# Layer 1 of a two-layer kernel in 13 chunks of 488 and 416 tokens instead of 14 chunks of 448

## The chip, the cores and the metric

The kernel runs on one core of one Trainium2 chip. The metric is the device time of one execution in microseconds (us); the number compared is the median of several runs. Beside the runs there is one execution with the hardware profiler on.

## The reference, cut to what matters

Two samples of 3136 tokens with 256 features go through three stages, one after the other:

```
scores = z @ z.T / 3136;  x = u * (max(scores, 0)**2 @ v)        # attention, no softmax
u = x + (x.T @ U @ V).T;  x = u + max(u @ w1a, 0) @ w2a          # layer 1, U and V of rank 32
u = x + real(fft2(x));    n = (u - mean) / sqrt(var + 1e-6)      # layer 2
out = u + max(n @ w1b, 0) @ w2b
```

The hidden width is 1024. All is float32. U, V and the four weight matrices come as 64-bit floats and are turned into 32-bit ones on the chip.

## The kernel before

Tokens and features stand in an order made on the host, so that the Fourier transform over 3136 = 64 x 49 tokens splits into small matmuls. Features lie on partitions (two halves of 128, called a), tokens along the free dimension. To keep float32 accuracy, every operand is split into a high part h and a remainder l (types that one pass of TensorE takes), and a product is three matmuls: high x high, high x low, low x high.

**Attention** (function `attention`, lines 423 to 826) walks over 14 query chunks of 448 tokens and 13 key blocks each. Its PSUM pools are given back at its end. The jobs that turn 64-bit numbers into 32-bit ones (`words`, line 158) run beside it. The first chunk of layer 1 is prepared in its last steps (`first_chunk`, line 706; lines 808 to 814).

**Layers 1 and 2** (lines 832 to 1187) are one loop over 28 chunks of 448 tokens: layer 1, sample 0, chunks 0 to 6; sample 1, chunks 0 to 6; then the same for layer 2. Each chunk has 8 steps, one for each 128 hidden units, and the loop variable i counts the 224 steps (line 1148). In step i `hidden` (line 363) does six matmuls for the chunk's hidden block (lines 368 to 370), ScalarE takes the ReLU (373) and VectorE the remainder (374). `project` (line 378) does the six matmuls back to 256 features (393 to 395) for the step two before, so that two steps lie between. Nothing is scheduled by the compiler here: the order of the program is the order on each engine's queue (`manual_schedule`).

What has to be done beside this is written as generators that advance once in every step, or as single calls at listed steps:

- `prep1` (line 260) and `prep2` (line 299) get the next chunk ready; they are put in at step 2 of a chunk's 8 for layer 1 and step 0 for layer 2 (line 1163). `prep1` does two matmuls of the low-rank term (269), adds the tokens (270) and splits the sum. `load` (252) brings the V columns of a chunk by two DMAs on the POOL queue.
- `mixer` (866) forms the rank-32 sums of sample 1, with the sample's own tile as a staging buffer.
- `halves49` (895) has four parts for each eighth of a sample: `fold`, `fetch`, `tokens` and `axis49`, at the steps of lines 1138 to 1143. `fold` reads tokens that layer 1 has finished.
- `fourier` (960) does the rest of the transform of one sample and adds it to the tokens. It starts at step 65 for sample 0 and 121 for sample 1 (line 1131), and rests in step 0 of each chunk. Line 1164 asserts that it is over when the first layer-2 chunk of its sample is prepared.
- `convert` (1092) turns the second layer's weights; `weights2` (1117) brings the second half of them in, from step 107.

DMAs go out on three queues: SP (`load`), POOL (`late_dma`) and, at few places, ACT. Attention writes its output to DRAM, and `load_x` (863) brings it back into the tiles `xT` (one for each sample, line 840) at the steps of lines 1146 and 1147.

## Time and profile before

| | |
|---|---|
| median of 3 runs | 1132.9 us (1132.52 to 1133.41) |
| the profiled execution | 1132.07 us |
| its span, first to last instruction | 1130.3 us |
| TensorE (PE) busy | 1125.1 us |
| VectorE (DVE) busy | 847.0 us |
| ScalarE (ACT) busy | 633.7 us |
| GpSimd (POOL) busy | 181.5 us |
| attention, to the first matmul of layer 1 | 536.7 us |
| layer 1, to the first matmul of layer 2 | 298.3 us |

All times inside the span count from its start. PE is the matmul itself, PEld the load of its weights, which runs beside other matmuls. A matmul's printed duration is modelled and overlaps the next one. A row of the timeline gives start, length, engine, line, operation, tiles (written <- read) and shape; "x6" at its end says that six like instructions were merged.

### The profile page before, as it was taken

What the parts mean: (1) busy time and instruction counts of PE and PEld (TensorE: products, weight loads), DVE (VectorE), ACT (ScalarE), POOL (GpSimd) and SP (SyncE); (2) the same over time, 40 slices, a digit from 0 to 9 for tenths busy, and PEclk for the clock granted to TensorE, in tenths of its full rate; (3) what the DMA queues carried; (4) which work ended last, traced back from release to release, by engine and by line L of the source; (5) the groups of instructions that cost most, each with busy time, mean ns of one, the idle gap of its engine ahead of it and who ended that gap; (6) DMA issues with size and microseconds to landing.
All of it is one profiled execution on the core that took longest, in us unless ns stands there. A gap on an engine that the chain in (4) does not pass through costs nothing.

```text
span 1130.3 us, 21424 instructions
## 1 busy us (share of the span) xinstructions
PE 1125.1 (100%) x8310; PEld 1061.7 (94%) x8310; DVE 847.0 (75%) x1571; ACT 633.7 (56%) x1032; POOL 181.5 (16%) x299
## 2 busy tenths in 40 slices
PE   9999999999999999999999999999999999999998
PEld 8999999999999999999989999999999999999997
DVE  8877888888887667676667777577588888777863
ACT  8777777878786666675334444343345444444431
POOL 2202310221022102202221112111131100000010
PEclk9999999999999999999999999999999999999999
DMA  5212322324123302111823455231143321111111
GB/s 168 75 46 61 104 80 69 119 71 127 47 72 118 121 18 59 50 36 32 265 62 95 128 159 130 74 75 45 47 107 100 76 48 42 33 42 33 42 33 42
DMA packets 86758, 88.96 MB, mean 79 GB/s; under 512 B 27398, under 2 KB 76034, under 8 KB 86656
## 3 DMA queue, kind: packets, MB, share of 16 engines
q1 hardware_dynamic: 70272, 58.44, 17.2%
q0 software_dynamic: 16032, 28.93, 10.2%
q8 instruction: 65, 1.06, 0.4%
q14 instruction: 37, 0.30, 0.1%
q10 hardware_dynamic: 352, 0.21, 0.1%
HBM read 57.67 MB, written 29.82 MB: 77 GB/s over the span
## 4 chain that ended last, share of the span: by engine, by line
PE 99%; ACT 0%; DVE 0%; issue 0%; DVEq 0%; POOL 0%; POOLq 0%
PE psO L616 37%; PE psS L574 9%; PE psH L368 8%; PE psH L369 8%; PE psC L394 8%; PE psC L395 8%; PE psH L370 8%; PE psC L393 8%; PE psS L743 0%; PE ps_m L995 0%; PE ps_g L995 0%; PE ps_x L995 0%; PE psS L234 0%; PE ps_g L234 0%; PE ps_m L958 0%; PE ps_m L957 0%
## 5 line engine op out<-in xcount | busy, mean ns | idle before, releaser
L616 PE MATMUL psO<-h,Vt 64*128 64x448 f32 x2744 | 345.1, 363 | 0.2 <-DVE h L585 0.2
L616 PEld LDWEIGHTS psO<-h,Vt 64*128 64x128 f32 x2744 | 294.4, 185 | 9.1 <-DVE h L585 0.7
L93 DVE TENSOR_TENSOR l<-P,h 128x896 fp32r<-128x896 f32 (+2 forms) x237 | 224.8, 954 | 33.3 <-ACT h L90 16.4
L373 ACT ACTIVATE Hh<-psH 128x448 fp32r<-128x448 f32 x224 | 121.0, 541 | 201.5 <-PE psH L370 198.3
L374 DVE SCALAR_TENSOR_TENSOR Hl<-psH,Hh 128x448 fp32r<-128x448 f32 x224 | 138.3, 620 | 117.9 <-ACT Hh L373 115.7
L590 ACT ACTIVATE P<-psS 128x896 f32<-128x896 f32 (+1 forms) x181 | 160.2, 885 | 85.4 <-PE psS L574 84.6
L616 PE MATMUL psO<-l,Vt 64*128 64x448 f32 x1372 | 206.4, 363 | 0.0
L592 DVE CAST h<-P 128x896 fp32r<-128x896 f32 (+1 forms) x181 | 110.9, 613 | 85.0 <-ACT P L591 83.8
L591 ACT ACTIVATE P<-P 128x896 f32<-128x896 f32 (+1 forms) x181 | 167.4, 925 | 5.7
L368 PE MATMUL psH<-h,w 128*128 128x448 f32 x448 | 166.5, 372 | 0.0
L616 PEld LDWEIGHTS psO<-l,Vt 64*128 64x128 f32 x1372 | 159.9, 185 | 4.4 <-DVE l L93 0.3
L369 PE MATMUL psH<-l,w 128*128 128x448 f32 x448 | 163.4, 365 | 0.0
L394 PE MATMUL psC<-Hl,w 128*128 128x448 f32 x448 | 163.4, 365 | 0.0
L370 PE MATMUL psH<-h,w 128*128 128x448 f32 x448 | 162.9, 364 | 0.0
L393 PE MATMUL psC<-Hh,w 128*128 128x448 f32 x448 | 162.9, 364 | 0.0
L395 PE MATMUL psC<-Hh,w 128*128 128x448 f32 x448 | 162.7, 363 | 0.0
L574 PE MATMUL psS<-Q,KT 64*128 64x448 f32 x1002 | 147.6, 364 | 0.0
L574 PEld LDWEIGHTS psS<-Q,KT 64*128 64x128 f32 x1002 | 115.2, 185 | 3.7 <-issue 0.4
L368 PEld LDWEIGHTS psH<-h,w 128*128 128x128 f32 x448 | 84.3, 188 | 7.9 <-issue 0.3
L393 PEld LDWEIGHTS psC<-Hh,w 128*128 128x128 f32 x448 | 84.2, 188 | 6.8 <-issue 0.2
L370 PEld LDWEIGHTS psH<-h,w 128*128 128x128 f32 x448 | 84.2, 188 | 6.5
L394 PEld LDWEIGHTS psC<-Hl,w 128*128 128x128 f32 x448 | 84.2, 188 | 6.3 <-DVE Hl L374 0.5
(313 smaller groups left out, 1157.1 us busy)
## 6 DMA issues: line engine op xcount, KB each, us to landing
out<-P SPq DMA_DIRECT2D x27, 224.0 KB, 1.9
uT<-in_uT SPq DMA_DIRECT2D x13, 448.0 KB, 4.0
aTd<-aT POOLq DMA_DIRECT2D x13, 448.0 KB, 3.1
aNd<-aT POOLq DMA_DIRECT2D x104, 56.0 KB, 2.4
vraw<-in_v SPq DMA_DIRECT2D x18, 256.0 KB, 2.7
scr<-wst SPq DMA_DIRECT2D x16, 256.0 KB, 2.0
Vs<-Vd POOLq DMA_DIRECT2D x28, 112.0 KB, 2.6
xT<-aTd SPq DMA_DIRECT2D x7, 448.0 KB, 4.6
```

The source lines that it names most:

```text
L93: tt(out=o, in0=a, in1=b, op=ALU.subtract)
L368: mm(ps[:, 0:CH], wh, self.h[:, a], start=a == 0, stop=False)
L369: mm(ps[:, 0:CH], wh, self.l[:, a], start=False, stop=False)
L370: mm(ps[:, 0:CH], wl, self.h[:, a], start=False, stop=a == 1)
L374: stt(out=l, in0=ps[:, 0:CH], scalar=0.0, in1=f(h), op0=ALU.max, op1=ALU.subtract)
L393: mm(dst, wh, h, start=k == 0, stop=False)
L394: mm(dst, wh, l, start=False, stop=False)
L395: mm(dst, wl, h, start=False, stop=k == 7)
L574: mm(dst[:, 0:w], k, q[r, kq, o : o + w], start=(kk, kq) == (0, 0), stop=kk == 1)
L590: act(out=A[:, x].rearrange("p (a n) -> p a n", a=2), in_=ps[:, :, 0:w], func=AF.Relu, scale=1.0 / S)
L591: act(out=A[:, x], in_=A[:, x], func=AF.Square)
L616: mm(o[fa][i][:, 0:CH], vt[r, j, k, fa * 128 : fa * 128 + 128], x[r, j * CH : j * CH + CH], start=p == 0 and fa not in [t[1][0] for t in t ...
```

## The change

Layer 1 takes both samples as one row of 6272 tokens and cuts it into 13 chunks, twelve of 488 and the last of 416. Chunk 6 holds the last 208 tokens of sample 0 and the first 280 of sample 1; its low-rank term is two matmuls for each half of the features, and its V columns come by four DMAs. Layer 2 keeps its 14 chunks of 448.

Both samples lie in one tile X, of which `xT` are views. Tiles that hold a chunk grow from 448 to 488 columns a half. For that, room is made elsewhere: the exponent of `words` is written into the lowest 16 bits of each 64-bit word instead of a separate stretch, the staging tiles shrink from 1152 to 1024 words, and the tiles `top`, `alt` and one of the two `wst` buffers move into the tile of U, which is free by then.

Layer 1 has 104 steps instead of 112. `fourier(0)` stays at step 65, `fourier(1)` moves from 121 to 113 and `weights2` from 107 to 99. The steps of the folds are listed one by one: for sample 0 they were 14, 22, 30, 38, 46, 54, 57, 58 and for sample 1 70, 78, 86, 94, 102, 110, 113, 114.

```diff
@@ -21,6 +21,8 @@
 N1, N2 = 64, 49
 CH = 448
 NC = S // CH
+CW = 488
+L1 = -(-NB * S // CW)
 NP = 13
 KPOS = 25
 
...
@@ -98,13 +100,13 @@
     dram = ctx.enter_context(tc.tile_pool(name="dram", bufs=1, space=DRAM))
 
     def ctile(tag, dt=F32, **k):
-        return com.tile([128, 2 * CH], dt, tag=tag, name=tag, **k)
+        return com.tile([128, 2 * CW], dt, tag=tag, name=tag, **k)
 
     def ptile():
         return ctile("P", bufs=4)
 
-    def c2(t):
-        return t.rearrange("p (a n) -> p a n", a=2)
+    def c2(t, n=CH):
+        return t.rearrange("p (a n) -> p a n", a=2)[:, :, 0:n]
 
     def run(gen):
         for _ in gen:
...
@@ -161,7 +163,7 @@
         hi = w.rearrange("p (n w) -> p n w", w=2)[:, :, 1]
         r16 = w.bitcast(U16).rearrange("p (n w) -> p n w", w=4)
         s, m = (raw[0:np_, k * n : k * n + n] for k in (2, 3))
-        e = raw[0:np_, 4 * n : 4 * n + n // 2].bitcast(U16)
+        e = r16[:, :, 0]
         nc.vector.tensor_scalar(out=e, in0=r16[:, :, 3], scalar1=0x7FF0, scalar2=None, op0=ALU.bitwise_and)
         nc.vector.tensor_scalar(out=m, in0=hi, scalar1=0xFFFFF, scalar2=None, op0=ALU.bitwise_and)
         yield
...
@@ -247,27 +249,36 @@
     class Chunk:
         def __init__(self, layer, b, c):
             self.layer, self.b, self.c = layer, b, c
-            self.sl = slice(c * CH, c * CH + CH)
+            t0 = b * S + c * CH if layer == 2 else c * CW
+            self.n = CH if layer == 2 else min(CW, NB * S - t0)
+            self.sl = slice(t0, t0 + self.n)
+            self.parts = []
+            for q in range(NB):
+                s, t = max(t0, q * S), min(t0 + self.n, q * S + S)
+                if s < t:
+                    self.parts.append((q, slice(s - t0, t - t0), slice(s - q * S, t - q * S)))
 
         def load(self):
-            self.vs = com.tile([128, CH], F32R, tag="Vs", name="Vs", bufs=1)
+            self.vs = com.tile([128, CW + 8], F32R, tag="Vs", name="Vs", bufs=1)
             for k in (0, 64):
-                late_dma(out=self.vs[k : k + 64, :], in_=V_d[:, self.sl])
+                for _, here, there in self.parts:
+                    late_dma(out=self.vs[k : k + 64, here], in_=V_d[:, there])
 
         def prep(self):
             return self.prep1() if self.layer == 1 else self.prep2()
 
         def prep1(self):
-            b, vs = self.b, self.vs
-            a = late["xT"][b][:, :, self.sl]
-            yield
-            if self.c or self.b:
+            n, vs = self.n, self.vs
+            a = late["X"][:, :, self.sl]
+            yield
+            if self.c:
                 yield
-            x, h, l = c2(ptile()), c2(ctile("h", F32R)), c2(ctile("l", F32R))
+            x, h, l = c2(ptile(), n), c2(ctile("h", F32R), n), c2(ctile("l", F32R), n)
             for k in range(2):
                 ps = misc()
-                mm(ps[:, 0:CH], Gs[b][:, k * 128 : k * 128 + 128], vs, start=True, stop=True)
-                tt(out=x[:, k], in0=ps[:, 0:CH], in1=a[:, k], op=ALU.add)
+                for b, here, _ in self.parts:
+                    mm(ps[:, here], Gs[b][:, k * 128 : k * 128 + 128], vs[:, here], start=True, stop=True)
+                tt(out=x[:, k], in0=ps[:, 0:n], in1=a[:, k], op=ALU.add)
                 hcopy(h[:, k], x[:, k])
                 sub(l[:, k], x[:, k], f(h[:, k]))
                 yield
...
@@ -362,16 +373,17 @@
 
         def hidden(self, k):
             w, mp = late["w"][self.layer][0], late["mp"]
-            ps = late["psH"].tile([128, 512], F32, tag="H", name="psH")
+            n = self.n
+            ps = late["psH"].tile([128, 512], F32, tag="H", name="psH")[:, 0:n]
             for a in range(2):
                 wh, wl = w.first(k, 0, a), w.first(k, 1, a)
-                mm(ps[:, 0:CH], wh, self.h[:, a], start=a == 0, stop=False)
-                mm(ps[:, 0:CH], wh, self.l[:, a], start=False, stop=False)
-                mm(ps[:, 0:CH], wl, self.h[:, a], start=False, stop=a == 1)
-            h = mp.tile([128, CH], F32R, tag="Hh", name="Hh", bufs=3)
-            l = mp.tile([128, CH], F32R, tag="Hl", name="Hl", bufs=3)
-            act(out=h, in_=ps[:, 0:CH], func=AF.Relu)
-            stt(out=l, in0=ps[:, 0:CH], scalar=0.0, in1=f(h), op0=ALU.max, op1=ALU.subtract)
+                mm(ps, wh, self.h[:, a], start=a == 0, stop=False)
+                mm(ps, wh, self.l[:, a], start=False, stop=False)
+                mm(ps, wl, self.h[:, a], start=False, stop=a == 1)
+            h = mp.tile([128, CW], F32R, tag="Hh", name="Hh", bufs=3)[:, 0:n]
+            l = mp.tile([128, CW], F32R, tag="Hl", name="Hl", bufs=3)[:, 0:n]
+            act(out=h, in_=ps, func=AF.Relu)
+            stt(out=l, in0=ps, scalar=0.0, in1=f(h), op0=ALU.max, op1=ALU.subtract)
             self.hid = getattr(self, "hid", {})
             self.hid[k] = (h, l)
 
...
@@ -389,7 +401,7 @@
                     parts.insert(1, self.held)
             for a, k, h, l in parts:
                 wh, wl = w.last(k, 0, a), w.last(k, 1, a)
-                dst = self.acc[a][:, 0:CH]
+                dst = self.acc[a][:, 0 : self.n]
                 mm(dst, wh, h, start=k == 0, stop=False)
                 mm(dst, wh, l, start=False, stop=False)
                 mm(dst, wl, h, start=False, stop=k == 7)
...
@@ -400,7 +412,12 @@
             b = self.b
             if self.layer == 1:
                 for a in range(2):
-                    tt(out=late["xT"][b][:, a, self.sl], in0=self.acc[a][:, 0:CH], in1=self.x[:, a], op=ALU.add)
+                    tt(
+                        out=late["X"][:, a, self.sl],
+                        in0=self.acc[a][:, 0 : self.n],
+                        in1=self.x[:, a],
+                        op=ALU.add,
+                    )
             else:
                 o = c2(ptile())
                 if self is chunks[-1]:
...
@@ -415,9 +432,9 @@
                     tt(out=o[:, a], in0=self.acc[a][:, 0:CH], in1=self.rs, op=ALU.mult)
                 for a in range(2):
                     tt(out=o[:, a], in0=o[:, a], in1=self.x[:, a], op=ALU.add)
-                    load(out=out[b, a * 128 : a * 128 + 128, self.sl], in_=o[:, a])
-
-    chunks = [Chunk(y, b, c) for y in (1, 2) for b in range(NB) for c in range(NC)]
+                    load(out=out[b, a * 128 : a * 128 + 128, self.c * CH : self.c * CH + CH], in_=o[:, a])
+
+    chunks = [Chunk(1, 0, c) for c in range(L1)] + [Chunk(2, b, c) for b in range(NB) for c in range(NC)]
 
 
     def attention(stack):
...
@@ -706,15 +725,16 @@
         def first_chunk(a):
 
             ch = chunks[0]
-            x = c2(ptile())
+            n = ch.n
+            x = c2(ptile(), n)
             for k in range(2):
                 ps = psS.tile([128, 2, 512], F32, tag="S", name="psS")
                 for i, r in enumerate(halves):
-                    mm(ps[:, i, 0:CH], Gs[0][r, k * 128 : k * 128 + 128], ch.vs[r], start=True, stop=True)
+                    mm(ps[:, i, 0:n], Gs[0][r, k * 128 : k * 128 + 128], ch.vs[r, 0:n], start=True, stop=True)
                 for i, y in enumerate((a, x)):
-                    tt(out=x[:, k], in0=ps[:, i, 0:CH], in1=y[:, k], op=ALU.add)
-            yield
-            h, l = c2(ctile("h", F32R)), c2(ctile("l", F32R))
+                    tt(out=x[:, k], in0=ps[:, i, 0:n], in1=y[:, k], op=ALU.add)
+            yield
+            h, l = c2(ctile("h", F32R), n), c2(ctile("l", F32R), n)
             for k in range(2):
                 hcopy(h[:, k], x[:, k])
                 sub(l[:, k], x[:, k], f(h[:, k]))
...
@@ -807,8 +827,8 @@
                 if (b, qc) == (1, NC - 1):
                     if p == 2:
                         chunks[0].load()
-                        a = att.tile([128, 2, CH], F32, tag="uT", name="uT")
-                        load(out=a, in_=aT_d[0][:, :, 0:CH].rearrange("a p n -> p a n"))
+                        a = att.tile([128, 2, CW], F32, tag="uT", name="uT")
+                        load(out=a, in_=aT_d[0][:, :, 0:CW].rearrange("a p n -> p a n"))
                     if n == NP - 3:
                         assert low_rank not in active
                         active.append(first_chunk(a))
...
@@ -837,7 +857,8 @@
     psX = ctx.enter_context(tc.tile_pool(name="psX", bufs=1, space=PSUM))
     misc_pools.extend([(psX, "m"), (psX, "x")])
 
-    xT = late["xT"] = [xpool.tile([128, 2, S], F32, tag=f"xT{b}", name=f"xT{b}") for b in range(NB)]
+    X = late["X"] = xpool.tile([128, 2, NB * S], F32, tag="xT", name="xT")
+    xT = [X[:, :, b * S : b * S + S] for b in range(NB)]
 
 
     raw128 = mp.tile([128, 112], F32, tag="raw128", name="raw128", bufs=1)
...
@@ -845,7 +866,13 @@
     rows = [mp.tile([128, CH], F32, tag=f"row{k}", name=f"row{k}", bufs=1) for k in range(2)]
     late["half"] = rows[0][:, 0:D]
     y = mp.tile([128, 416], F32, tag="y", name="y", bufs=1)
-    top = [mp.tile([98, 32], F32, tag=f"top{b}", name=f"top{b}", bufs=1) for b in range(NB)]
+    spare = Us.rearrange("p a n -> p (a n)")
+    top = [spare[0:98, 768 + 32 * b : 800 + 32 * b] for b in range(NB)]
+    stored = [0]
+
+    def wst():
+        stored[0] += 1
+        return spare[:, 0:512] if stored[0] % 2 else mp.tile([128, 512], F32, tag="wst", name="wst", bufs=1)
     for t in (raw128, col128, y[:, 392:416]):
         nc.gpsimd.memset(t, 0.0)
 
...
@@ -867,11 +894,11 @@
 
         g = psX.tile([128, 512], F32, tag="g", name="ps_g")[:, 0:D]
 
-        raw = xT[1].rearrange("p a n -> p (a n)")
-        blocks = [raw[:, s * D : s * D + D] for s in range(24)] + [late["half"]]
+        raw = [xT[1][:, s // 12, s % 12 * D :] for s in range(0, 24, 4)]
+        blocks = [r[:, j * D : j * D + D] for r in raw for j in range(4)] + [late["half"]]
         for s in range(0, 24, 4):
             load(
-                out=raw[:, s * D : (s + 4) * D].rearrange("p (s d) -> p s d", s=4),
+                out=raw[s // 4][:, 0 : 4 * D].rearrange("p (s d) -> p s d", s=4),
                 in_=aN_d[1][128 * s : 128 * s + 512].rearrange("(s p) d -> p s d", p=128),
             )
             if s == 16:
...
@@ -926,7 +953,7 @@
         def alternating(i, x):
 
             v = x[0:98].rearrange("p (s d r) -> p s d r", s=4, r=2)
-            t = mp.tile([98, 4, 64], F32, tag="alt", name="alt", bufs=1)
+            t = spare[0:98, 512:768].rearrange("p (s d) -> p s d", s=4)
             sub(t, v[:, :, :, 0], v[:, :, :, 1])
             nc.vector.reduce_sum(out=top[b][0:98, 4 * i : 4 * i + 4], in_=t, axis=mybir.AxisListType.X)
 
...
@@ -946,7 +973,7 @@
         def axis49(i):
             ps = misc()
             dft49(ps, *nat.pop(i))
-            w = mp.tile([128, 512], F32, tag="wst", name="wst")
+            w = wst()
             hcopy(w, ps)
             load(out=scr[b][:, 4 * i : 4 * i + 4, :], in_=w.rearrange("p (s d) -> p s d", s=4))
 
...
@@ -1128,17 +1155,19 @@
         active = []
         mix1, last = mixer(), chunks[-1].prep()
         starts = {
-            4: mix1, 1: convert(0), 3: convert(1), 65: fourier(0), 121: fourier(1), 107: weights2(),
+            4: mix1, 1: convert(0), 3: convert(1), 65: fourier(0), 113: fourier(1), 99: weights2(),
         }
-        calm = [starts[65], starts[121]]
+        calm = [starts[65], starts[113]]
 
         events, folds = {}, {}
         for b in range(NB):
             ops = halves49(b)
             for k in range(8):
-                at = (b * NC + k) * 8 + 14 if k < 6 else b * NC * 8 + 51 + k
+                done = -(-(b * S + 392 * k + 392) // CW) - 1
+                at = (14, 22, 30, 38, 46, 49, 53, 58, 70, 78, 82, 86, 94, 102, 105, 106)[8 * b + k]
+                assert at >= 8 * done + 9
                 go = max(at + 2, 36 + 2 * k)
-                wait = b == 0 and k in (4, 5)
+                wait = b == 0 and k in (4, 5, 6)
                 for op, j in zip(ops, (at, go, go + 2 + wait, go + 4 + wait)):
                     (folds if op is ops[0] else events).setdefault(j, []).append((op, k))
 
...
@@ -1161,11 +1190,11 @@
             if i == 0:
                 chunks[1].load()
             if c + 2 < len(chunks) and k == 4 - 2 * chunks[c + 1].layer:
-                assert not (c + 1 == 2 * NC and calm[0] in active or c + 1 == 3 * NC and calm[1] in active)
+                assert not (c + 1 == L1 and calm[0] in active or c + 1 == L1 + NC and calm[1] in active)
                 active.insert(0, chunks[c + 1].prep())
             if i == 8:
                 chunks[2].load()
-            if k == 6 and 0 < c < 2 * NC - 2:
+            if k == 6 and 0 < c < L1 - 2:
                 chunks[c + 2].load()
             if i in starts:
                 active.append(starts[i])
```

## Rows read from the trace of the kernel before

**Rows 1.** The page, busy time by engine and the granted clock in 40 slices

```profile
PE 1125.1 (100%) x8310; PEld 1061.7 (94%) x8310; DVE 847.0 (75%) x1571; ACT 633.7 (56%) x1032; POOL 181.5 (16%) x299
...
PEclk9999999999999999999999999999999999999999
```

**Rows 2.** The page, the chain that ended last, by engine and by line

```profile
PE 99%; ACT 0%; DVE 0%; issue 0%; DVEq 0%; POOL 0%; POOLq 0%
PE psO L616 37%; PE psS L574 9%; PE psH L368 8%; PE psH L369 8%; PE psC L394 8%; PE psC L395 8%; PE psH L370 8%; PE psC L393 8%; PE psS L743 0%; PE ps_m L995 0%; PE ps_g L995 0%; PE ps_x L995 0%; PE psS L234 0%; PE ps_g L234 0%; PE ps_m L958 0%; PE ps_m L957 0%
```

**Rows 3.** Groups: line, engine, tiles, shape, count, busy us, mean ns, idle before

```profile
L373 ACT ACTIVATE Hh<-psH 128x448 fp32r<-128x448 f32 x224 | 121.0, 541 | 201.5 <-PE psH L370 198.3
L374 DVE SCALAR_TENSOR_TENSOR Hl<-psH,Hh 128x448 fp32r<-128x448 f32 x224 | 138.3, 620 | 117.9 <-ACT Hh L373 115.7
...
L370 PEld LDWEIGHTS psH<-h,w 128*128 128x128 f32 x448 | 84.2, 188 | 6.5
```

**Rows 4.** Timeline of PE in layer 1, first matmul of a chunk and of the next

```profile
597.47 0.37 PE L368 MATMUL psH<-h,w 128*128 128x448 f32 x1
...
617.28 0.36 PE L368 MATMUL psH<-h,w 128*128 128x448 f32 x1
```

**Rows 5.** Timeline of PE, three matmuls of 512 columns and the next

```profile
785.84 0.39 PE L956 MATMUL ps_m<-nh,b49h 128*128 128x512 f32 x1
...
786.53 0.37 PE L269 MATMUL ps_x<-Vs,Gs 128*128 128x448 f32 x1
```

**Rows 6.** Timeline of PE, six matmuls of 384 columns and the next

```profile
728.80 0.33 PE L1013 MATMUL ps_m<-Th,fA 128*128 128x384 f32 x1
...
729.84 0.36 PE L368 MATMUL psH<-h,w 128*128 128x448 f32 x1
```

**Rows 7.** Timeline where attention ends, DVE and PE

```profile
535.20 1.34 DVE L93 TENSOR_TENSOR l<-P,h 128x448 fp32r<-128x448 f32 x2
...
536.73 0.47 PE L368 MATMUL psH<-h,w 128*128 128x448 f32 x1
...
537.65 0.36 PE L369 MATMUL psH<-l,w 128*128 128x448 f32 x1
```

**Rows 8.** Groups of DVE: integer words, and two strided inputs

```profile
L165 DVE TENSOR_SCALAR stg<-stg 128x256 uint16<-128x256 uint16 (+3 forms) x25 | 7.1, 285 | 0.0
...
L93 DVE TENSOR_TENSOR alt<-nl 98x256 f32<-98x256 f32 x16 | 6.7, 417 | 2.2 <-DMA nl<-natd 2.2
```

**Rows 9.** Timeline of SP and DVE in layer 1; last, issues by size and landing

```profile
562.71 0.47 SPq L864 DMA_DIRECT2D xT<-aTd  x1
...
569.93 0.62 DVE L270 TENSOR_TENSOR P<-ps_x,xT 128x448 f32<-128x448 f32 x1
...
xT<-aTd SPq DMA_DIRECT2D x3, 896.0 KB, 10.1
```

**Rows 10.** Windows: length, then PE, PEld, DVE, ACT, POOL busy (count), clock, DMA

```profile
706.00:787.00 81.00, 81.00 (x428) 75.42 (x427) 53.92 (x119) 30.40 (x67) 12.17 (x21) 1.00 0.26 65
...
861.90:955.00 93.10, 93.10 (x491) 86.85 (x490) 79.31 (x179) 42.37 (x97) 11.89 (x22) 1.00 0.23 60
```

**Rows 11.** Timeline, late matmuls in layer 2 and in layer 1

```profile
927.07 0.62 DVE L374 SCALAR_TENSOR_TENSOR Hl<-psH,Hh 128x448 fp32r<-128x448 f32 x1 [1.09 <-ACT Hh L373]
...
927.75 0.47 PE L394 MATMUL psC<-Hl,w 128*128 128x448 f32 x1
928.06 0.36 PE L395 MATMUL psC<-Hh,w 128*128 128x448 f32 x1
...
762.56 0.34 PE L1015 MATMUL ps_m<-Th,fA 128*128 128x384 f32 x1
...
763.12 0.34 PE L1017 MATMUL ps_x<-Tl,fB 128*128 128x384 f32 x1
```

**Rows 12.** Timeline of PE in attention, six half-height matmuls of 224 columns

```profile
20.59 0.49 PE L574 MATMUL psS<-Q,KTl 64*128 64x224 f32 x6
20.92 0.98 PE L616 MATMUL psO<-h,Vt 64*128 64x448 f32 x8
```

14 lines of the change are left out of this document (8 added, 6 removed).

## The prediction

> **What bounds the kernel now.** I read the page first. TensorE is busy for 1125.1 of 1130.3 us and its granted clock stands at 9 or more tenths of full speed, the 2.4 GHz level, in every slice [rows 1]. Busy time of a pipelined engine can hide gaps, so the chain of waits came next: 99% of it is PE, and the six matmul lines of the two layers have 8% each [rows 2]. No DMA and no other engine ends a stage. The third view was the groups of instructions: each of the six lines has 448 matmuls with a weight load each, 224 steps with two per line, and a load takes 188 ns, shorter than the distance of two matmuls found below, so it is covered [rows 3]. What counts is then that distance from start to start, and it is read from the timeline, since a printed duration is modelled and overlaps the next. In one undisturbed chunk of layer 1 the first matmul starts at 597.47 us and the one that opens the next chunk at 617.28, with 98 matmuls between (12 in each of 8 steps and two for the low-rank term): 19.81 us / 98 = 202.1 ns [rows 4]. 448 columns at 2.4 GHz are 186.7 ns, so each matmul takes some 15 ns more than one tick for each column.
>
> **What the change takes away.** Layer 1 does 14 chunks x 96 = 1344 matmuls of 448 columns; then it does 12 x 96 = 1152 of 488 and 96 of 416. The columns are equal (6272 x 96), the count falls by 96. Only a part of the time that does not grow with columns can be saved, so I need the distance at 488. Three matmuls of 512 start at 785.84 and the next instruction at 786.53: 230 ns each [rows 5]. Six of 384 run from 728.80 to 729.84: 173.3 ns each [rows 6]. Between 448 and 512 a column costs (230 - 202.1)/64 = 0.436 ns, between 384 and 448 (202.1 - 173.3)/64 = 0.450 ns; one tick of the granted clock is 0.417 ns. Two readings follow.
> By the rows: 488 costs 202.1 + 40 x 0.436 = 219.5, 416 costs 202.1 - 32 x 0.450 = 187.7. 1344 x 202.1 = 271.6 us; 1152 x 219.5 + 96 x 187.7 = 252.9 + 18.0 = 270.9. Saved: 0.7 us.
> By the tick: 488 costs 218.8, 416 costs 188.8; 252.1 + 18.1 = 270.2. Saved: 1.4 us.
> I take the reading by the rows, **0.7 us saved**: both sides of 448 have a row of their own, and neither shows the tick as the price of a column. A rounding of 10 ns over three matmuls moves the 512 by 3.3 ns, the 488 by 2.1 and the sum by 2.4 us, which gives the outer bounds: 3.1 us saved to 1.7 us lost by this term alone.
>
> A rule speaks against even this. The Trainium skill, TensorE: Matmul & The Clock Gate, section Back-to-back issue gap, gives for an isolated matmul at full clock N/2.4 plus about 2.5 ns. By it, as an estimate, 96 fewer matmuls would save 0.24 us. The trace disagrees with it in the level, 15 ns above the columns instead of 2.5 at 448, and the measurement decides.
>
> The part that doesn't grow is smaller than those 15 ns by the rows: 0.7 us / 96 is 7 to 8 ns a matmul.
>
> **What the rest of the edits cost.** The matmuls of the low-rank term in layer 1 stay 26: twenty of 488, two of 416, and the chunk across the samples has two pairs of 208 and 280. Their columns are the same but for the first chunk; below 0.05 us. V loads on the POOL queue stay 28 (13 chunks with two and two more for the split one). I count zero.
> The first chunk is prepared while attention ends. Its DVE and ACT work grows by 40 columns, at most 620/448 x 40 = 55 ns an instruction [rows 3], seven on the path: 0.4 us. Its last split ends at 536.54 us, and the second matmul with it starts at about 537.65, four matmuls and more behind the first at 536.73 [rows 7]: 1.1 us of cover, so nothing; without the cover 0.4 us.
> A step of layer 1 grows by 12 x 17 = 0.2 us on TensorE. ReLU (541 ns) and its remainder (620 ns) grow by 9%, together 0.1 us [rows 3], and their reader comes two steps later. They gain room.
> The integer words of the conversions: the exponent is written with a step of four 16-bit words in place of densely. The input already has that step, and 285 ns for 256 elements is already one element at a time [rows 8]. I take nothing; the bound from above is the row with two strided inputs, 417 ns, 132 more for each of 41 instructions, 5 us of VectorE, which is 75% busy [rows 1] and off the chain [rows 2].
> Both samples in one tile could add waits between a load into one sample and arithmetic on the other. Loads and arithmetic of one sample already share a tile: a load of 896 KB is issued at 562.71 and takes some 10.1 us to land, yet an add that reads other columns of that tile runs at 569.93 [rows 9]. Regions are told apart, so I take nothing. The same holds for the spare rows of the U tile, which take over two small tiles and one of two store buffers; depth stays two.
> Steps written out by hand: the first Fourier block keeps step 65, but layer 1 is eight steps shorter. By its yields and the skipped steps it ends in step 95, and the first layer-2 preparation begins in step 96, where eight free steps lay between. One more fold and its transforms fall into its run (steps 82 to 92). The stores, loads and SP issues of a fold move with it; no queue gets more of them. In 706 to 787 us, where the block runs now, VectorE is busy 53.9 of 81 us and ScalarE 30.4 [rows 10]; there is room. The second Fourier block and the second weights move eight steps with the layer's end, so layer 2 meets them as before.
>
> **Sum.** Profiled execution: 1132.07 us around a span of 1130.3; less 0.7 is 1131.4. The median of the runs shown is 0.8 higher, 1132.9, and the prediction goes by it: **1132.2 us**. A measurement can tell this kernel from an unchanged one at about 0.2%, 2.3 us; the forecast is below that.
>
> **The rivals.**
> A, more than counted: layer 1's odd stalls go too, as the longer step gives ScalarE and VectorE more room. For it: such a stall exists. A late remainder runs from 927.07 to 927.69, and the matmul that reads it, at 927.75, holds up the next to 928.06, 0.1 us more than usual [rows 11]. In layer 1 two matmuls of 384 take from 762.56 to 763.12, 0.21 us more than two of 173.3 ns [rows 11], and I estimate all such places of the layer at twice this, 0.4 us. Against: they have their own causes in a few steps, and the steps stay. With the tick's 1.4 that is 1.8 us, 1131.1, and the outer bound above, 3.1 us, would give 1129.8.
> B, nothing fixed is saved: the 15 ns grow with the columns, as rate and not as a constant (202.1/448 x 488 = 220.1; 1152 x 220.1 + 96 x 187.7 = 271.6). Then 1132.9. For it: 230/512 = 0.449 and 202.1/448 = 0.451 are nearly one rate, and so is 173.3/384 = 0.451. Against: no row shows why a column should cost more than a tick, and the step from 448 to 512 is a little short of the rate. The page's 2.5 ns, weighed above, ends next to this, at 1132.7.
> C, slower: the squeeze of the first Fourier block. Place: step 95 to 104. If its last adds come late, the first layer-2 chunk is not split when step 104 opens. It decides when the delay exceeds the two steps (5 us) between its split and its use; each step beyond costs 2.6 us. Two lost: 1132.9 - 0.7 + 5.2 = 1137.4. For it: the second block in layer 2 runs at 79.3 of 93.1 us of VectorE [rows 10] and gives the stall above. Against: that stall cost 0.1 us, and 0.1 us stalls would have to come 30 times to undo 0.7 us and add 2.3.
> D, slower: TensorE takes columns in whole groups and 488 costs as 512. 1152 x 230 + 96 x 202.1 = 284.4, 12.7 us more: 1145.6. Against: three pairs with 224 columns take 0.33 us, 110 ns a pair [rows 12], 224 ticks (93) and 15 ns, not 256 ticks (107) and 15. Groups of 32 stay open.
>
> **Numbers.** Forecast 0.45, B 0.23, A 0.17, C 0.10, D 0.05. Faster by over 0.2% (below 1130.6): the part of A that lies towards its outer bound and a little of the forecast's spread, 0.12. Slower: D and half of C, 0.10. The rest, 0.78, is within. The range goes from near A's bound, 1130.0, to 1134.6, the forecast's outer bound (1132.9 + 1.7); C with two steps and D lie outside.
>
> **What would show it.** Right: an undisturbed layer-1 chunk of 98 matmuls lasts 98 x 219.5 = 21.5 us instead of 19.81; layer 1, 298.3 us now, from 536.73 [rows 7] to the first matmul of layer 2, is shorter by about 0.7 us; attention and layer 2 keep their lengths; the six lines have 27 x 16 = 432 matmuls each. B shows 220 ns, D 230. C shows as a gap before the first matmul of layer 2. Wrong: attention or layer 2 changing by over 1 us, which no step above allows.

## The result: 1139.5 us, 0.6% slower

| | before | after |
|---|---|---|
| median, 6 runs each on the same chip | 1132.71 us (1131.77 to 1133.41) | 1139.47 us (1139.40 to 1140.28) |
| ratio, 95% interval | | 1.0062 (1.0052 to 1.0073) |
| the profiled execution | 1132.07 us | 1139.42 us |
| span of the profiled execution | 1130.3 us | 1137.7 us |
| attention, to the first matmul of layer 1 | 536.73 us | 536.58 us |
| layer 1, to the first matmul of layer 2 | 298.32 us | 301.83 us |
| layer 2, to the end | 295.25 us | 299.25 us |

The forecast was 1132.2 us with a range to 1134.6; the result lies outside it and on the other side. The span grew by 7.4 us: 3.5 in layer 1, and 4.0 in layer 2, where the change left the work as it was.

The page of the changed kernel (busy time, clock, chain by engine, two groups):

```profile
span 1137.7 us, 21201 instructions
PE 1130.0 (99%) x8214; PEld 1035.8 (91%) x8214; DVE 847.8 (75%) x1557; ACT 634.2 (56%) x1022; POOL 180.6 (16%) x299
PEclk9999999999999999999999999999999999999999
PE 92%; issue 2%; DVE 2%; DMA 2%; ACT 1%; SPq 0%; DVEq 0%; POOL 0%; ACTq 0%; POOLq 0%
L385 ACT ACTIVATE Hh<-psH 128x448 fp32r<-128x448 f32 (+2 forms) x216 | 120.0, 556 | 204.1 <-PE psH L382 199.3
L386 DVE SCALAR_TENSOR_TENSOR Hl<-psH,Hh 128x448 fp32r<-128x448 f32 (+2 forms) x216 | 136.9, 637 | 119.8 <-ACT Hh L385 117.7
```

The clock still stands at its upper level in every slice [rows 1], and PE has 96 matmuls less (8214 in place of 8310), yet is busy longer. In the chain PE has lost 7 points [rows 2] to other engines, DMA and issue, so some wait has come onto it. But a chain that ends in matmuls says nothing of matmuls that have each become longer. That is read from start to start, as before. Layer 1, the first matmuls of two chunks with 98 between them, changed kernel:

```profile
602.67 0.38 PE L380 MATMUL psH<-h,w 128*128 128x488 f32 x1
624.43 0.38 PE L380 MATMUL psH<-h,w 128*128 128x488 f32 x1
```

21.76 us / 98 = 222.0 ns for 488 columns; 219.5 was forecast. In layer 2 the same two rows, first of before, then of after:

```profile
966.15 0.36 PE L368 MATMUL psH<-h,w 128*128 128x448 f32 x1
985.88 0.36 PE L368 MATMUL psH<-h,w 128*128 128x448 f32 x1
```

```profile
971.31 0.37 PE L380 MATMUL psH<-h,w 128*128 128x448 f32 x1
991.22 0.37 PE L380 MATMUL psH<-h,w 128*128 128x448 f32 x1
```

19.73 us against 19.91: 201.3 and 203.2 ns, for the same 448 columns and operations and at the same clock. Over all of layer 2's 1344 matmuls 2 ns are 2.7 us or more. Below, "quiet distance" is the mean distance of neighbouring matmuls in such stretches, from some 600 rows of the timeline (190 in layer 1); it is 201.18 ns in before and 203.51 in after for layer 2, 202.2 and 222.05 for layer 1.

Two words for what follows. A matmul reads two operands: its weights, a block of 128 columns, and the moving operand, the 448 or 488 columns that are multiplied with them. The matmuls that write psH take the chunk tile as moving operand and the first weights; those that write psC take the hidden tiles Hh and Hl and the second weights. The place of an operand is its start address in bytes, as the built program has it; the traces don't hold it.

The wait on the chain, in the timeline of the changed kernel (SPq is SP's queue issuing a DMA):

```profile
669.16 0.57 SPq L891 DMA_DIRECT2D xT<-aTd  x1
670.43 0.16 DVE L937 TENSOR_TENSOR y<-xT 128x8 f32<-128x8 f32 x1
...
674.60 0.63 DVE L937 TENSOR_TENSOR y<-xT 128x192 f32<-128x192 f32 x2 [4.01 <-DMA xT<-aTd]
674.64 0.39 PE L405 MATMUL psC<-Hh,w 128*128 128x488 f32 x1
675.80 1.20 DVE L386 SCALAR_TENSOR_TENSOR Hl<-psH,Hh 128x488 fp32r<-128x488 f32 x2
676.48 0.49 PE L406 MATMUL psC<-Hl,w 128*128 128x488 f32 x1 [1.45 <-DVE Hl L386]
```

A fold of sample 0 waits 4.01 us for a load into sample 1, which it does not read. The two remainders (L386) queued behind it on VectorE come late, and PE goes from 674.64 to 676.48, 1.84 us in place of 0.22.

### The profile page after: what moved, and what is told of

The parts are those of the page before. It is cut to its first block, busy times and chain, and to the rows that moved or that the text cites. A ratio compares the mean times of both kernels' runs of the same rounds, so it can differ in the third digit from the quotient of the medians.

```text
span 1137.7 us, 21201 instructions
## 1 busy us (share of the span) xinstructions
PE 1130.0 (99%) x8214; PEld 1035.8 (91%) x8214; DVE 847.8 (75%) x1557; ACT 634.2 (56%) x1022; POOL 180.6 (16%) x299
## 4 chain that ended last, share of the span: by engine, by line
PE 92%; issue 2%; DVE 2%; DMA 2%; ACT 1%; SPq 0%; DVEq 0%; POOL 0%; ACTq 0%; POOLq 0%
PE psO L633 35%; PE psS L591 9%; PE psC L406 7%; PE psH L380 7%; PE psH L381 7%; PE psH L382 7%; PE psC L407 7%; PE psC L405 7%; DMA xT<-aTd 0%; DMA vraw<-in_v 0%; PE ps_x L1022 0%; PE ps_m L1022 0%; DMA natd<-yt 0%; DVE Hl L386 0%; ACT P L607 0%
## 5 line engine op out<-in xcount | busy, mean ns | idle before, releaser
L633 PEld LDWEIGHTS psO<-h,Vt 64*128 64x128 f32 x2744 | 278.2, 184 | 12.9 <-DVE h L602 1.1
L95 DVE TENSOR_TENSOR l<-P,h 128x896 fp32r<-128x896 f32 (+4 forms) x235 | 224.5, 960 | 32.7 <-ACT h L92 15.9
L385 ACT ACTIVATE Hh<-psH 128x448 fp32r<-128x448 f32 (+2 forms) x216 | 120.0, 556 | 204.1 <-PE psH L382 199.3
L386 DVE SCALAR_TENSOR_TENSOR Hl<-psH,Hh 128x448 fp32r<-128x448 f32 (+2 forms) x216 | 136.9, 637 | 119.8 <-ACT Hh L385 117.7
L633 PE MATMUL psO<-l,Vt 64*128 64x448 f32 x1372 | 191.5, 362 | 0.1
L380 PE MATMUL psH<-h,w 128*128 128x448 f32 (+2 forms) x432 | 163.9, 379 | 0.0
L406 PE MATMUL psC<-Hl,w 128*128 128x448 f32 (+2 forms) x432 | 161.5, 374 | 1.6 <-DVE Hl L386 1.6
L381 PE MATMUL psH<-l,w 128*128 128x448 f32 (+2 forms) x432 | 161.7, 374 | 0.0
L382 PE MATMUL psH<-h,w 128*128 128x448 f32 (+2 forms) x432 | 161.4, 374 | 0.0
L407 PE MATMUL psC<-Hh,w 128*128 128x448 f32 (+2 forms) x432 | 161.0, 373 | 0.0
L405 PE MATMUL psC<-Hh,w 128*128 128x448 f32 (+2 forms) x432 | 161.0, 373 | 0.0
L633 PEld LDWEIGHTS psO<-l,Vt 64*128 64x128 f32 x1372 | 145.1, 184 | 6.3 <-DVE l L95 0.5
```

Source lines behind the costliest of these rows:

```text
L95: tt(out=o, in0=a, in1=b, op=ALU.subtract)
L380: mm(ps, wh, self.h[:, a], start=a == 0, stop=False)
L381: mm(ps, wh, self.l[:, a], start=False, stop=False)
L382: mm(ps, wl, self.h[:, a], start=False, stop=a == 1)
L386: stt(out=l, in0=ps, scalar=0.0, in1=f(h), op0=ALU.max, op1=ALU.subtract)
L405: mm(dst, wh, h, start=k == 0, stop=False)
```

## The experiments

Times are medians, each ratio is to runs of before on the same chip (their medians lie between 1132.48 and 1133.41 us).

### The false wait, and the layout of after

**Split loads.** Each load of tokens is written as two DMAs, one for each half of the features:

```diff
-        load(out=xT[b][:, :, s:e], in_=aT_d[b][:, :, s:e].rearrange("a p n -> p a n"))
+        for a in range(2):
+            load(out=xT[b][:, a, s:e], in_=aT_d[b][a, :, s:e])
```

> The changed kernel, in which each load of attention's output into X goes out as two DMAs, one for each half of the features, so that what it writes is one stretch of X and not two with the other sample between. Theory (the fold of sample 0 waits for a load into sample 1 that only seems to overlap): the 4.0 us wait of the fold in step 46 and the 1.6 us gap of TensorE at 674.6 us are gone, 1137.8 us. Rival (the fold reads what that load brings, or waits for SP's queue): the gap stays, 1139.5 us.

It took 1137.28 us, ratio 1.0043 (1.0028 to 1.0058). The fold waits no more; timeline of this run, the load and the fold:

```profile
668.47 1.06 SPq L892 DMA_DIRECT2D xT<-aTd  x2
669.77 0.70 DVE L938 TENSOR_TENSOR y<-xT 128x8 f32<-128x8 f32 x3
```

The chunk around it shrinks from 24.18 to 22.46 us, by 1.7. Both quiet distances stay at 203.51 and 222.05. So the wait was false: the fold reads nothing that this load writes, and two loads that each keep to one half of X don't hold it up. Between the two halves of sample 1's columns lie sample 0's of the second half; that the one wide load was taken to cover them is the reading that fits, not a measurement. The rest of the loss is another thing.

**Aligned to 64 bytes.** In after a chunk tile's halves are 1952 bytes apart, in before 1792, which is 7 x 256. Here 496 columns (1984 bytes):

```diff
-        return com.tile([128, 2 * CW], dt, tag=tag, name=tag, **k)
+        return com.tile([128, 2 * 496], dt, tag=tag, name=tag, **k)
```

(the hidden tiles Hh and Hl likewise, and one store buffer for two)

> The changed kernel with the halves of its chunk tiles 496 columns apart instead of 488, and the hidden tiles 496 columns each, so that every moving operand of the layers' matmuls starts on a multiple of 64 bytes; the second store buffer is given up to make room. Theory (a matmul takes longer when moving operands start 32 bytes off a multiple of 64): the distance of quiet layer-2 matmuls falls from 203.5 to 201.2 ns and that of the 488-column ones from 221.7 to about 219.5; 1152 x 2.2 + 1344 x 2.2 = 5.5 us less, 1134.0 us. Rival (the distance grows by rate with the columns, or by where the weights lie): 488 stays at 221.7, layer 2 at 203.5, 1139.5 us.

It took 1138.8 us, 1.0059 (1.0042 to 1.0076), with quiet distances of 202.83 ns in layer 2 and 220.93 in layer 1. Of the 2.33 ns that layer 2's distance had grown by, 0.68 are back. That fits a dependence on places, but a multiple of 64 bytes is not the rule.

**The layout alone, in before.** Halves and hidden tiles 456 columns apart, 448 used; no other part of the change, but that the small tiles `top` and `alt` go into the U tile, to make room:

```diff
-        return com.tile([128, 2 * CH], dt, tag=tag, name=tag, **k)
+        return com.tile([128, 2 * 456], dt, tag=tag, name=tag, **k)
-            h = mp.tile([128, CH], F32R, tag="Hh", name="Hh", bufs=3)
+            h = mp.tile([128, 456], F32R, tag="Hh", name="Hh", bufs=3)[:, 0:CH]
```

> The kernel before with 448-column chunks as they are, but the halves of its chunk tiles 456 columns apart and the hidden tiles 456 columns each, so that about half of the moving operands start 32 bytes off a multiple of 64, as in the changed kernel; two small tiles go into the U tile to make room. Theory of the start addresses: quiet matmuls go from 201.2 to about 203.5 ns in both layers, 2688 x 2.2 = 5.9 us more, 1138.6 us. Rival (the 488 columns or the single tile for both samples are the cause): 201.2 ns and 1132.7 us.

It took 1136.74 us, 1.0036 (1.0023 to 1.0049). One chunk of layer 2 in this run:

```profile
969.16 0.37 PE L368 MATMUL psH<-h,w 128*128 128x448 f32 x1
989.14 0.36 PE L368 MATMUL psH<-h,w 128*128 128x448 f32 x1
```

19.98 us / 98 = 203.9 ns; over the stretch the quiet distance is 203.25. The chunks and the matmuls are those of before, so this shows the second cause by itself. Its control, `top` and `alt` moved and nothing else:

> The control for the two runs made from the kernel before: only the two small tiles are put into the U tile, no operand of a layer's matmuls changes its residue to 256 bytes except the hidden tiles. All theories: within 0.5 us of the kernel before, 1132.8 us, 201.2 ns. If it is slower by 2 us or more, the move of the small tiles and not the pitch made the 456-column run slow.

It took 1132.21 us, 0.9999 (0.9989 to 1.0009), with a distance of 201.18: the room made costs nothing.

**Pitches of 512 columns in after**, with split loads; all operands of the layers' matmuls stand at the same places modulo 256 bytes as in before (two of three `wr` buffers are left, one of two `wst`).

> The changed kernel with the loads into X split by feature half, the halves of the chunk tiles 512 columns (2048 bytes) apart and the hidden tiles 512 columns each, so that all moving operands and weights have the residues to 256 bytes that they have in the kernel before; one store buffer and one Fourier staging buffer fewer, to make room. Theory, widened (the places of the operands to 256 bytes or more set the distance, not only to 64): quiet matmuls of layer 2 fall from 203.5 to 201.2 ns, those of 488 columns from 221.7 to 219.5; with no false wait 1139.5 - 1.7 - 5.5 = 1132.3 us. Rival (what the wider chunk moves elsewhere, or 488 itself, costs): 203 and 221 to 222 ns, about 1137 us.

It took 1138.14 us, 1.005 (1.0035 to 1.0065). Layer 2's quiet distance is 201.18 again, to the hundredth of a ns, though the run has stalls of its own, one of 2.2 us at 928.85, where PE waits for a load into one of the fewer `wr` buffers. A chunk of layer 1:

```profile
604.59 0.38 PE L380 MATMUL psH<-h,w 128*128 128x488 f32 x1
626.28 0.38 PE L380 MATMUL psH<-h,w 128*128 128x488 f32 x1
```

21.69 us / 98 = 221.3 ns, and the quiet distance is 221.45: with the places of before, 488 columns are still dearer than the 219.5 of the forecast.

**512 columns** in this layout (`CW = 512`), to price the columns:

> The kernel after in the layout with pitches of 512 columns and split loads, now with chunks of 512 tokens: twelve of 512 and one of 128. It prices a 512-column matmul in the main loop in the same layout in which 488 cost 221.45 and 448 cost 201.2 to 202.2 ns. Theory (a rate per column of about 0.454 ns): 512 x 0.454 = 232 ns, 1152 x 232 + 96 x 58 = 273 us for layer 1's matmuls, as with 488. Rival (a fixed part and a tick per column: 202.2 + 64 x 0.417): 229 ns, 269.5 us, 3.5 less. The run by the theory about 1138, by the rival about 1135.

It took 1142.47 us, 1.0081 (1.0061 to 1.0101). Timeline, chunk to chunk:

```profile
606.51 0.40 PE L380 MATMUL psH<-h,w 128*128 128x512 f32 x1
629.17 0.40 PE L380 MATMUL psH<-h,w 128*128 128x512 f32 x1
```

22.66 us / 98 = 231.2 ns, 0.4516 for a column, as 202.2 / 448 = 0.4513. It is nearer the rate (232) than the tick (229). 1152 x 231.2 are 266.3 us, and by the rate the last 96 of 128 columns would make it 271.9, against 1344 x 202.2 = 271.8. The run came out 4.5 us above the 1138 that were expected. Its last chunk took 13.11 us: the matmuls of 128 columns are some 112 ns apart and not 58 (twelve of the chunk's matmuls still belong to the 512-column chunk ahead of it). So small a matmul is bound by something else, which was not looked into.

**Two shifts.** In after the V tile is made 64 bytes longer (one store buffer), which moves the weights and the hidden tiles by 64 and leaves the chunk tiles; and in before all tiles are moved by 32:

> The changed kernel with the V tile 64 bytes longer, which moves every weight tile behind it by 64 bytes, from 64 off a multiple of 128 to a multiple of 128; the moving operands keep their places to 64 bytes; one store buffer instead of two. Theory of the moving operand's start: nothing changes, 203.5 ns and 1139.5 us. Rival (the weights' start is the cause): 201.2 ns, about 1134 us.

It took 1140.12 us, 1.0066 (1.0046 to 1.0086), with 203.26 ns in layer 2 and 221.65 in layer 1: no help.

> The kernel before with a gap of 32 bytes ahead of the tiles, so that every moving operand and every weight tile of attention and of the layers lies 32 bytes off a multiple of 64 while all distances between them stay; two small tiles go into the U tile to make room. Theory of the absolute start (32 bytes off costs 2 ns): 203 ns in both layers, 1138 us, and attention longer too. Rival (only the places relative to each other count): 201.2 ns, 1132.8 us.

It took 1133.96 us, 1.0014 (1.0005 to 1.0023), yet with quiet distances of 201.09 and 202.2: where the whole begins doesn't count, how tiles stand to one another may.

**The store buffer in the U tile**, put into before:

> The kernel before, with the two small tiles and one of the two store buffers in spare rows of the U tile, as the change has them; operand places modulo 256 bytes stay those of before. It asks whether the store buffer in the U tile makes the stall of about 0.5 us at the opening of layer 2. If it does: a matmul gap of 0.4 to 0.7 us within the first two steps of layer 2, and the run about 1133.3 us. If it does not: no such gap, 1132.7, and the stall belongs to the eight steps that layer 1 lost. In both cases the quiet distance of layer 2 stays at 201.2 ns.

It took 1133.43 us, 1.0 (0.999 to 1.001), without a gap there. After has a stall of some 0.5 us as layer 2 opens (862.72 to 863.33); this edit is not its cause, and it stays open which other edit is.

### Which tile's place counts

**The hidden tiles alone at 456 columns, then the chunk tiles alone:**

> The kernel before with one thing changed: the two hidden tiles Hh and Hl are 456 columns wide in memory (448 used), so their buffers begin at different places modulo 256 bytes; the chunk tiles keep multiples of 256 bytes. Theory (the place of the matmul's own moving operand modulo 256 bytes sets its distance): the 6 matmuls of a step that read Hh and Hl go from 201 to about 203 ns, the 6 that read the chunk stay at 201; the mean of layer 2's quiet stretch about 202.2, the run 1134 to 1135.5 us. Rival (any uneven pitch slows every matmul alike): all 12 at about 203.2, the run 1136 to 1137. Rival (only the chunk's halves matter): 201.2 in all, 1132.7.

It took 1137.07 us, 1.0035 (1.0023 to 1.0048), with 202.87 ns in layer 2.

> The kernel before with the other half of that layout alone: the halves of a chunk tile lie 456 columns apart, the hidden tiles keep one place modulo 256 bytes. Theory: the 6 matmuls of a step that read the chunk go to about 203 ns, the 6 that read Hh and Hl stay at 201; mean about 202.2, the run 1134 to 1135.5 us, and its loss and that of the run with wider hidden tiles add up to the 4.0 us of both together. Rival (any uneven pitch slows every matmul alike): 203.2, 1136 to 1137. Rival (only the hidden tiles matter): 201.2, 1132.7.

It took 1134.17 us, 1.0008 (0.9999 to 1.0018), with 202.42 ns: 203.2 in the psH matmuls and 201.6 in the psC ones, as the theory said (the weights and hidden tiles behind the chunk tiles moved as well, those of the psC matmuls together). In the run before it the theory failed: the psH matmuls, whose moving operands had stayed, took 202.8 too. But the wider hidden tiles had pushed other tiles on, and with them the second layer's first weights, from 192 to 128 modulo 256. All runs from here on that start from before have `top` and `alt` in the U tile, as the control. The next two take weights and hidden tiles apart with a pad, the first in the kernel before, the second with the hidden tiles wide:

```diff
-                return late["mp"].tile([128, CH], F32, tag=f"A{k + 1}", name=f"A{k + 1}", bufs=1)
+                return late["mp"].tile([128, CH + 48 * k], F32, tag=f"A{k + 1}", name=f"A{k + 1}", bufs=1)[:, 0:CH]
```

(16 for 48 in the second)

> The kernel before with only the second layer's first weights (those whose matmuls write psH) at another place: 128 modulo 256 bytes in place of 192, as in the run with wider hidden tiles; all moving operands keep the places of before (0 and 64). Theory W (the weights' place counts too): the psH matmuls of layer 2's quiet stretch go from 201.35 to about 202.8 ns, the psC ones stay at 201.0, the run about 1133.5 us. Rival (only moving operands count): 201.2 in both, 1132.7. Layer 1, whose weights do not move, stays at 202.2 under both.

It took 1133.62 us, 1.001 (1.0001 to 1.002). One step of layer 2, its first psH matmul, its first psC, and the psC matmul six later:

```profile
986.97 0.37 PE L368 MATMUL psH<-h,w 128*128 128x448 f32 x1
...
988.19 0.37 PE L393 MATMUL psC<-Hh,w 128*128 128x448 f32 x1
...
989.40 0.36 PE L393 MATMUL psC<-Hh,w 128*128 128x448 f32 x1
```

Six psH take 1.22 us here, six psC 1.21. Over the quiet stretch psH went from 201.35 to 203.2 ns, psC from 201.0 to 201.5, layer 1 stayed at 202.2.

> The hidden tiles 456 columns wide as before, but the second layer's first weights put back to 192 modulo 256 bytes. Theory W: the psH matmuls of layer 2's quiet stretch come back from 202.8 to about 201.5 ns, the psC ones, which read the hidden tiles, stay at 203; mean 202.2. Rival (only the hidden tiles count, for all matmuls): 202.9 in both groups again, 1137 us.

It took 1137.1 us, 1.0036 (1.0022 to 1.005). The same three rows:

```profile
970.74 0.36 PE L368 MATMUL psH<-h,w 128*128 128x448 f32 x1
...
971.94 0.37 PE L393 MATMUL psC<-Hh,w 128*128 128x448 f32 x1
...
973.17 0.37 PE L393 MATMUL psC<-Hh,w 128*128 128x448 f32 x1
```

1.20 us for the six psH, 1.23 for the six psC; over the stretch 201.3 and 203.5. So the place of the weights counts as well as that of the moving operand, and in layer 2 mostly for their own matmuls. In layer 1 it does not keep to them: there the psH matmuls, whose two operands stand as in before, went from 202.6 to 203.9 ns when only the hidden tiles became wider (203.7 over both kinds). That accounts for layer 1, which was 2.0 us longer than in before; attention was 1.8 us longer without a known cause. So the run's time stayed at 1137.

**All of layer 2's operands at 0 modulo 256**, by two such pads:

> The kernel before with all operands of layer 2's matmuls at 0 modulo 256 bytes: chunk tiles, hidden tiles and both weights. Theory (aligned places are what makes 201.2): 201.2 or a little less, 1132.7 us or a little below. Rival (what counts is how the places stand to one another, and before's 0, 64 and 192 were a good set): 202 to 203.5 in layer 2, 1135 to 1137.

It took 1137.53 us, 1.0046 (1.0031 to 1.0061), with layer 2 at 203.7 ns: perfectly aligned, and as slow as after. One of its chunks:

```profile
970.06 0.36 PE L368 MATMUL psH<-h,w 128*128 128x448 f32 x1
990.22 0.37 PE L368 MATMUL psH<-h,w 128*128 128x448 f32 x1
```

That is 20.16 us / 98 = 205.7 ns, while other chunks of the same run, at the same places modulo 256, take as little as 202.6. What sorts the matmuls is thus not the place of either operand but, as far as this goes, how the two stand to each other. Grouped by (start of the moving operand - start of its weights) modulo 256, the 448-column matmuls of the quiet stretches of twelve kernels read:

| difference, bytes | 0 | 32 | 64 | 96 | 128 | 160 | 192 | 224 |
|---|---|---|---|---|---|---|---|---|
| mean distance, ns | 203.2 | 204.7 | **201.5** | 204.9 | 203.1 | 203.2 | 202.4 | 203.2 |
| matmuls | 1560 | 235 | 3732 | 466 | 1245 | 290 | 487 | 447 |

These are means of mixed layouts, and they are no law: at a difference of 64 the single kernels range from 201.2 to 202.5 ns, at 192 from 201.1 to 203.3.

### The rule tried as a forecast, and a faster kernel

In before layer 2's matmuls stand at 64, layer 1's psC too, layer 1's psH and all of attention at 0. A rule found afterwards has to forecast something. **Both layers at 64**, by a pad of 48 columns behind the V tile and 16 behind A2:

```diff
-            self.vs = com.tile([128, CH], F32R, tag="Vs", name="Vs", bufs=1)
+            self.vs = com.tile([128, CH + 48], F32R, tag="Vs", name="Vs", bufs=1)[:, 0:CH]
```

> The kernel before with every matmul of both layers set so that its moving operand begins 64 modulo 256 bytes after its weights (chunk 0, weights 192, hidden tiles 0); in before the psH matmuls of layer 1 alone stood at 0. Theory (the difference of the two places decides): layer 1's psH matmuls go from 202.7 to about 201.3 ns, layer 1's quiet distance from 202.2 to 201.4, layer 2 stays at 201.2; 672 x 1.4 = 0.9 us, the run about 1131.8 us: the first version faster than before. Rival (absolute places count): layer 1 at 202.2 or more and layer 2 changed, since hidden tiles at 0 were slow in the run with all places at 0.

It took **1123.45 us, 0.9914 (0.99 to 0.9927)**, 9.9 us less where 0.9 were expected. Timeline, a chunk of layer 1:

```profile
592.61 0.36 PE L368 MATMUL psH<-h,w 128*128 128x448 f32 x1
612.23 0.36 PE L368 MATMUL psH<-h,w 128*128 128x448 f32 x1
```

19.62 us / 98 = 200.2 ns where before has 202.1 [rows 4]; layer 2 is at 200.03, too, which the theory had left at 201.2. Layer 1 is 2.3 us shorter, layer 2 1.3, and attention 4.5: the pad had also moved the weight tiles of attention's second product (Vt) to a difference of 64.

**Attention alone**, by a pad of 48 columns behind the last tile of its pool, which sets Vt and KT to 64 and leaves the layers as they were:

```diff
-            g = att.tile([128, D], F32, tag="G", name="G", bufs=1)
+            g = att.tile([128, D + 48], F32, tag="G", name="G", bufs=1)[:, 0:D]
```

> The kernel before with a pad in the last tile of attention's pool alone: its weight tiles (Vt, KT) stand at 192 modulo 256 bytes, their moving operands (chunk tiles, Q) at 0, so every attention matmul reads 64 after its weights; in before all stood at 0. The layers' tiles keep the places of before. Theory (the difference of places decides, for any matmul): attention 4 to 5 us shorter, 532 to 533 us, layer 1 298.4 and layer 2 295.3 as before, the run about 1128 us. Rival (attention's length varies from build to build, 535 to 538.5 so far, and the 4.5 us were that or the layers' doing): attention 535 or more, the run about 1132.7.

It took 1124.62 us, 0.9927 (0.9912 to 0.9942). The end of attention, and the first matmul of layer 1:

```profile
528.38 0.36 PE L616 MATMUL psO<-l,Vt 64*128 64x448 f32 x1
528.68 0.47 PE L368 MATMUL psH<-h,w 128*128 128x448 f32 x1
```

Layer 1 begins at 528.68 in place of 536.73 [rows 7], 8.0 us earlier where 4 to 5 were expected, and the layers are unchanged (298.65 and 295.25 us; 202.2 and 201.18 ns). The 4.5 us of the run before were thus no chance. The other 3.5 came with the places of the score matmuls, which stand at 64 here and stood at 0 there; whether the score matmuls alone got faster was not taken apart.

**All three together:**

> The version with both layers' moving operands 64 after their weights, which had the Vt weights of attention right and left the score matmuls (Q against KT) at a difference of 0; now these stand at 64 too. Theory: the score matmuls are 774 of some 3900 pairs' matmuls in attention; another 0.5 to 1.5 us off attention, the run 1122 to 1123. Rival (only matmuls with much of the time on them show it): 1123.45 again.

It took **1120.44 us, 0.9891 (0.9875 to 0.9908)**, span 1118.7: attention 528.73, layer 1 296.00, layer 2 293.92. It is faster than both kernels, with the old 14 chunks, `top` and `alt` in the U tile, and four pads that hold no data (V tile 48 columns, A2 16, and in attention G 48 and `qraw` 16).

**After with both layers at 64**, with its 512-column pitches and split loads:

> The kernel after with pitches of 512 columns and split loads, and the same places (moving operand 64 after its weights everywhere). Theory: layer 1's psH matmuls of 488 columns go from 223.3 to about 220 ns like its psC ones, layer 1's quiet distance from 221.45 to 220.0, layer 2 stays at 201.2; 1152 x 220.0 + 96 x 187.5 = 271.4 us against 1344 x 201.4 = 270.7 for before at the same places: fewer and wider matmuls still gain nothing. The run 1136 to 1137.5 us (it keeps the stalls of its fewer buffers). Rival (the part that doesn't grow is there, hidden by bad places): 219 or below and a gain of 1 us or more over before's 270.7.

It took 1131.87 us, 0.9988 (0.9979 to 0.9997). A chunk of layer 1:

```profile
601.57 0.38 PE L380 MATMUL psH<-h,w 128*128 128x488 f32 x1
623.14 0.38 PE L380 MATMUL psH<-h,w 128*128 128x488 f32 x1
```

21.57 us / 98 = 220.1 ns, and layer 2's quiet distance is 200.03. Now both sizes have equal places: 220.1 / 488 = 0.4510 for a column, 200.1 / 448 = 0.4467. 1152 x 220.1 + 96 x 187.5 = 271.6 us against 1344 x 200.1 = 268.9: wider chunks cost layer 1 2.7 us by this sum, and its length says 298.48 - 295.99 = 2.5. Attention is 3.7 us longer than in the run of before with both layers at 64 (535.90 against 532.23). Its products don't stand at a difference of 64 here (those with Vt at 192, the scores at 128), which fits, but no run tried it.

In the three runs with the chunks of before, the rule foretold the direction and not the size: 0.9, 4 to 5 and 0.5 to 1.5 us were expected, the last beyond the run with both layers, and 9.9, 8.0 and some 3 came. In the last run it foretold layer 1's distance (220.0) and missed layer 2's (201.2) and the time (1136 to 1137.5).

## Why the prediction was wrong

**Where the 7.4 us lie.** The forecast failed in three steps, named below. Layer 1: the false wait 1.7; the price of the columns with the places of before, 1152 x 221.45 + 96 x 187.7 - 1344 x 202.2 = 273.1 - 271.8 = 1.3; the uneven places 1152 x 0.6 = 0.7. Together 3.7, measured 3.5. Layer 2: 1344 x 2.33 = 3.1 for the places and some 0.5 for the stall at its opening: 3.6, measured 4.0.

**"Regions are told apart, so I take nothing" failed.** [Rows 9] show a load and an add on columns of one tile of one sample. In the joint tile X a load of sample 1 has two stretches, with sample 0's second half between them. Splitting the load removed the wait and 1.7 us.

**The tiles' pitch was no term of the sum.** The growth of the tiles from 448 to 488 columns was named only as room that had to be made. The prediction wrote that layer 2 changing by over 1 us would be wrong "which no step above allows"; that test fired. The run with the layout alone shows it, and the run with the old places gives the distance back.

**"I take the reading by the rows, 0.7 us saved" was mis-sized, in sign too.** 488 columns cost 221.45 ns with the places of before, not 219.5, and 1.3 us were lost. Rival B had the right mechanism, nothing fixed to save, and its 220.1 came nearest, still 1.3 short. This step alone would have stayed within the range, whose upper end was a loss of 1.7 us by this term; the wait and the pitch took the result out of it. The slope from one row at 512 in another stage (230, rounded to 10 ns in three) could not carry the choice between B and the forecast; their difference was 0.6 ns. The rule weighed there, of the Trainium skill, TensorE: Matmul & The Clock Gate, section Back-to-back issue gap, has a small fixed part per matmul, too; between 448 and 512 columns no run here shows one that can be saved.

**What held.** The counts (216 ReLUs, 96 matmuls fewer), the clock, attention's cover for the first chunk (536.58 against 536.73), the exponent's new step (VectorE 847.8 us against 847.0, with 14 instructions fewer). Rival C's place shows 0.5 us and not two steps; rival D's 230 ns for 488 did not come.

## What to carry to other kernels

When a tile's size changes, list where all tiles behind it come to lie: every matmul that reads a moved tile may have a new price, in stages that the change doesn't touch. A stage with unchanged work is the best witness: compare its matmul distance from start to start before anything else. And when two regions are put into one tile, look at the transfers whose pattern spans both, not at those with plain ranges.

## What the hardware showed that was not expected

In this kernel a matmul's distance depended on where its moving operand starts in relation to its weights, modulo 256 bytes: at 448 columns it was 200.0 ns with every pair of the layers at a difference of 64, 201.5 as the mean at 64 in the other layouts, 203 at 0 and 128, near 205 at 32 and 96, with the clock at its upper level throughout. With 64 set everywhere it was worth 12.6 us of 1133, in a kernel whose profile showed PE busy for 100%. The Trainium skill, SBUF — State Buffer, section Operand start alignment, asks only that an operand start at a multiple of its element size, and says that this is about what is allowed and not about speed; all the places here fulfil it, and their mean distances run from 200.0 to 204.9 ns.

The difference is not the whole of it: layer 2 stood at 64 in before and still went from 201.2 to 200.0 ns when hidden tiles and the other weights moved by 192 together. Contention with ScalarE's or VectorE's work does not explain the slow places: in after, the matmuls during which both are idle are as slow (203.3 ns, 25 of them) as those with both at work (203.0, 108). For the 1.2 ns by which before's layer 2 stood above 200.0 it is not excluded: there the idle ones took 200.0 ns (19 of them) and those with both at work 202.4 (89). What in the reading of the operands makes the 3 ns is open.
